# Turning a reversed block instead of copying mirrored filter rows: one change to a spectral filter that runs beside a gated MLP

## The chip, the cores and the metric

One NeuronCore of a Trainium2 chip runs the whole program. The metric is the device time of one execution in microseconds (us). Five engines work side by side, each on its own list of instructions in order: PE (TensorE, matrix products), DVE (VectorE), ACT (ScalarE), POOL (GpSimd) and SP (SyncE, which here only issues transfers). A lower time is better.

## The reference, cut to what matters

The output is the sum of the input, of a filter in the frequency domain and of a gated MLP, both on the layer-normed input. S is 2048 rows, D 512 columns, Df 1792; all arrays are bf16.

```python
def _A_ref(x, w_r, w_i):
    B, S, D = x.shape
    X = rfft2(x.astype(float32), axes=(-2, -1))
    W = w_r + 1j * w_i                       # (S, D // 2 + 1)
    X = X * W
    return irfft2(X, s=(S, D), axes=(-2, -1)).astype(bfloat16)

def _B_ref(x, w_gate, w_up, w_down):
    g = einsum("bsd,df->bsf", x, w_gate)
    u = einsum("bsd,df->bsf", x, w_up)
    h = gelu(g) * u
    return einsum("bsf,fd->bsd", h, w_down)

xn = layernorm(A_x, axis=-1)
return A_x + _A_ref(xn, A_w_r, A_w_i) + _B_ref(xn, B_w_gate, B_w_up, B_w_down)
```

## The kernel before

**A planner writes the order.** The program first records operations (`op`), each with an engine, a cost, a key and what it reads and writes. `_Sched.run` then walks through them with these costs, picks at each step the operation that can start first (the key decides between close ones, a `due` time overrides it), and adds `MARGIN`, 1 us, to the time at which a matmul counts as ready. What comes out is one fixed list for each engine. On the chip each engine follows its list; an instruction that finds its input missing holds everything behind it. So a changed cost or a new operation can move instructions that have nothing to do with it.

**The rows.** The 2048 rows are 16 tiles of 128, and four tiles make a block (blocks 0 to 3). For each tile `stats` (L524, L525) takes mean and variance, POOL or ACT makes the reciprocal root (L537, L531), and `norm` (L541) writes the normed rows to specB, in eight slots of 512 elements. A normed tile is transposed into xnT: tiles 0 to 3 on PE (`turn`, L554, copied out of PSUM in L559), tiles 4 to 15 by a transfer on SP's queue (`turn_dma`, L563).

**The MLP.** `gated` multiplies 128 rows of wg and of wu by xnT (L686, PE), ACT applies gelu (L691) and copies the other product (L692), and DVE multiplies both into hT (L693). gg and uu have four buffers each and ps_gu has three PSUM banks. Block 0 has 128-wide (`first`, L705) and 256-wide pieces first; all else is 512 wide. `down` (L731) multiplies by wd.

**The filter.** `fold` (L571) takes a block of xnT and makes the sums and differences of its four groups of 128 columns in f: two groups for the even channels, two for the odd ones; then it folds rows against their mirror rows into z (L584, L586). `f_c` (L597) multiplies z by cosines and sines (Tf): for each pair of tiles, two matmuls of 128 columns for the even channels and two of 256 for the odd ones, twice. ACT copies the result to specA (L602). When all 16 tiles are there, DVE does a 16-point transform across tiles (from L780 on), and PE the rest over 128 rows (`f_t`, L820 and L823). The spectrum X stands in eight classes of rows. For the product, DVE folds X to real and mirrored parts, multiplies by the filter W (`filt`, real and imaginary parts, near rows and mirrored "far" rows) in two halves of four classes each (L849 to L884), and PE and DVE go back the same way (`f_i` L900, L901; `f_b` L960), until the result is added to x and stored (L748). The last rows of the MLP (L731 into ps_sp) end the program.

**Transfers.** SP's queue carries, in this order: the x tiles and weights, the rest of `small` (288 KB of constants), x of blocks 2 and 3, four transposes, wd, six transposes, tokf, two transposes, then the filter. Its near rows are loaded straight (strided rows of 514 bytes). Its far rows are needed in reversed order: three transfers for each of w_r and w_i copy them reversed into a scratch tensor w_mirror in DRAM (L655 to L659), and six loads each bring them in from there. `toki`, constants for L900, stands between. The two small sums `edge` (L833, POOL) wait for the whole filter, and DVE uses them and W near the product.

```python
load("sp", small[:, 2:11].rs([9 * P]), c_small.ap()[:, 2 * P:], 294912, key=next(k))
...
for s in (2, 3):
    norm(s, -50.0)
    turn(s, 1, -50.0)
fold(0)
...
    turn_dma(s)
    if s % 4 == 3:
        fold(s // 4)
```

Of the kernel before, what the change touches and what calls it, by code (L numbers as in the profile page):

```python
# [9 lines left out]
BF16 = mybir.dt.bfloat16  # L10
# [3 lines left out]
D = 512  # L14
FF = 1792
P = 128
# [19 lines left out]

def _constants():
    npbf = mybir.dt.np(BF16)
    th = 2.0 * np.pi / S
    m = np.arange(P)  # L40
    K = np.zeros((8, P))
    K[0] = 8 * (2 * (m % 64) + m // 64)
    for v, c in enumerate((4, 1, 9, 2, 10, 3, 11)):
        K[v + 1] = c + 16 * m
    q = np.arange(P) + 0.5
    ph = th * q[:, None, None] * K[None]
    co, si = np.cos(ph), np.sin(ph)
    si2 = si.copy()
    si2[:, 0, 0] = np.sin(th * q * 1024)
    cof = co.copy()  # L50
    cof[:, 0, 0] *= 0.5
    low = (m < 64)[None]
    tf = []
    for a in (cof, si2):
        for part in (low, ~low):
            e = a[:64, 0] * part
            tf.append(np.concatenate([e, 0 * e] if a is cof else [0 * e, e]))
    for v, c in enumerate((4, 1, 9, 2, 10, 3, 11)):
        g = -1.0 if c > 8 else 1.0
        c = min(c, 16 - c)  # L60
        if c % 2:
            r = np.sin(np.pi * c / 2)
            f = r * g, r
        else:
            f = (-1.0, 1.0) if c == 4 else (g, -1.0)
        tf.append(np.concatenate([co[:64, v + 1], f[0] * si[:64, v + 1]]))
        tf.append(np.concatenate([g * co[:64, v + 1], f[1] * si[:64, v + 1]]))
    tf = np.stack(tf, 1)
    ci, sv = co[:64].transpose(2, 1, 0), si2[:64].transpose(2, 1, 0)
    sg = np.array([0, 1, 1, 1, 1, -1, -1, -1])[:, None]  # L70
    pr = np.concatenate([ci, -sg * sv], 2)
    pi = np.concatenate([sv, sg * ci], 2)
    lo = (m < 64)[:, None]
    for a in (pr, pi):
        half = a[:, 0, 0:64].copy()
        a[:, 0] = np.concatenate([half * lo, half * ~lo], 1)
    ti = np.stack([pr, pi, -pi], 2)
    a = 2.0 * np.pi / D * (np.arange(P) + 0.5)[:, None]
    ke = 2 * np.arange(P)[None]
    kse = ke.copy()  # L80
    kse[0, 0] = 256
    T = np.stack([np.cos(a * ke), np.cos(a * (ke + 1)), np.sin(a * kse), np.sin(a * (ke + 1))], 1)
    al = np.full((P, 4), 2.0)
    al[0, 0] = al[0, 2] = 1.0
    Ti = T.transpose(2, 1, 0) * al[:, :, None] / (S * D)
    fwd = []
    for d0, r in ((0, (0,)), (0, (2,)), (0, (1, 3)), (P, (1, 3))):
        kk = np.concatenate([np.arange(i, 256, 4) for i in r])[None]
        ks = np.where(kk == 0, 256, kk)
        a = 2.0 * np.pi / D * (d0 + np.arange(P) + 0.5)[:, None]  # L90
        fwd += [np.cos(a * kk), np.sin(a * ks)]
    small = np.concatenate([np.eye(P)] + fwd + [Ti.reshape(P, 512)], 1)

    def cvt(z):
        return np.ascontiguousarray(z.reshape(P, -1).astype(np.float32).astype(npbf))

    return cvt(small), cvt(tf), cvt(ti)
# [253 lines left out]
def bass_parallel_sum__spectral_gfnet__glu_gated_geglu__prompt_kernel(  # L351
# [26 lines left out]
    op = sch.op  # L378

    with ExitStack() as es:  # L380
# [22 lines left out]
        small = sb("smallc", [11, P])  # L403
        tf = sb("tokf", [18, P])
# [22 lines left out]
        Tf = small[:, 1:7]  # L427
        Ti = small[:, 7:11]
# [71 lines left out]
        load("sp", small[:, 2:11].rs([9 * P]), c_small.ap()[:, 2 * P:], 294912, key=next(k))  # L500
# [69 lines left out]

        def fold(b):  # L571
# [8 lines left out]
            tt(f[:, :, 2:4], xt[:, :, 0:2], xt[:, :, 2:4], SUB, 1024, kk)  # L580
# [6 lines left out]
            for p in {0: (), 1: (4, 6), 2: (8, 10), 3: (12, 14, 0, 2)}[b]:  # L587
                t = _T("sp")

                def f_c(e, p=p, t=t):  # L590
                    ins = None
                    for o in range(2):
                        bank = spb(t, o).rearrange("p (s r i) -> p s r i", s=2, r=4)
                        for cc in range(4):
                            to = bank[:, :, 2 * cc] if cc < 2 else bank[:, :, 1::2]
                            mat = Tf.ap[:, cc] if cc < 2 else Tf.ap[:, 2 * cc - 2:2 * cc]
                            ins = e.matmul(to, z.ap[:, p + o, cc, :], mat, start=(cc == 0), stop=(cc == 3))  # L597
                    return ins

                op("pe", 4 * 0.057 + 4 * 0.11, f_c, reads=(z[:, p:p + 2], Tf), tiles=(t,), key=kk, lag=0.1)  # L600
# [17 lines left out]
        for s in (2, 3):  # L618
            norm(s, -50.0)
            turn(s, 1, -50.0)  # L620
        fold(0)
# [5 lines left out]
        for s in range(4, 16):  # L627
            norm(s, 0.0, NORM[0] + NORM[1] * (s - 4))
            hold[s] = sch.ops[-1]
            turn_dma(s)  # L630
            if s % 4 == 3:
                fold(s // 4)
# [4 lines left out]
        load("sp", tf, c_tf.ap().rearrange("p (t m) -> p t m", t=18), 589824, key=next(k))  # L637
        for ri, src in ((0, A_w_r), (1, A_w_i)):
            r16 = src.rearrange("(m c) k -> m c k", c=16)
            load("sp", W[0:64, ri, 0, 0], r16[0:64, 0], 32896, key=next(k))  # L640
            load("sp", W[64:P, ri, 0, 0], r16[0:64, 8], 32896, key=next(k))
            load("sp", W[:, ri, 0, 1], r16[:, 4], 65792, key=next(k))
            for c in (1, 2, 3):
                load("sp", W[:, ri, 0, 2 * c:2 * c + 2], r16[:, c:c + 9:8], 131584, key=next(k))
            load("sp", W[0:1, ri, 1, 0], r16[0:1, 0], 514, key=next(k))
        op("pool", 0.1, lambda e: e.memset(w1[0:1].ap, 0.0), writes=(w1,))
        for dst, src, lo, hi in ((w1[0:1, 0, 0:256], A_w_r, 0, 256), (w1[0:1, 0, 257:512], A_w_i, 1, 256),
                                 (w1[0:1, 1, 1:256], A_w_i, 1, 256), (w1[0:1, 1, 257:512], A_w_r, 1, 256),
                                 (w1[0:1, 1, 256:257], A_w_r, 256, 257)):
            load("sp", dst, src[1024:1025, lo:hi], 512, key=next(k))  # L650
        gate.append(hold[15])
        scr, far, near = {}, {}, {}
        for ri, src in ((0, A_w_r), (1, A_w_i)):
            c16 = src.rearrange("(m c) k -> c m k", c=16)
            scr[ri] = nc.dram_tensor("w_mirror%d" % ri, (9, P, 257), BF16, kind="Internal").ap()  # L655
            far[ri] = [
                dma("sp", lambda ri=ri: scr[ri][0:4], lambda c16=c16: c16[12:16, ::-1, :], 526336, key=next(k), cost=3.5, lag=6.0),
                dma("sp", lambda ri=ri: scr[ri][5:8], lambda c16=c16: c16[5:8, ::-1, :], 394752, key=next(k), cost=2.5, lag=6.0)]
            near[ri] = dma("sp", lambda ri=ri: scr[ri][4:9:4, 0:64], lambda c16=c16: c16[0:9:8, 127:63:-1, :], 131584, key=next(k), cost=2.0, lag=5.0)  # L659
        load("sp", ti, c_ti.ap().rearrange("p (v t q) -> p v t q", v=8, t=3), 786432, key=next(k))  # L660
        for ri in (1, 0):
            load("sp", W[1:64, ri, 1, 0], scr[ri][4, 0:63], 32382, after=(near[ri],), key=1.0 + next(k))
            load("sp", W[64:P, ri, 1, 0], scr[ri][8, 0:64], 32896, after=(near[ri],), key=1.0 + next(k))
            load("sp", W[:, ri, 1, 1], scr[ri][0], 65792, after=(far[ri][0],), key=1.0 + next(k))
            for c in (1, 2, 3):
                load("sp", W[:, ri, 1, 2 * c:2 * c + 2], scr[ri][4 - c::4][0:2].rearrange("c m k -> m c k"), 131584, after=tuple(far[ri]), key=1.0 + next(k))
# [122 lines left out]
        u = Fb[:, 2:4]  # L789
        tt(u, s2[:, 0:2], s2[:, 2:4], ADD, 1024)  # L790
        tt(H[:, 14], u[:, 0], u[:, 1], ADD, 512)
        tt(H[:, 15], u[:, 0], u[:, 1], SUB, 512)
# [20 lines left out]
        for v, hh in enumerate(((14, 15), (12, 13), (0, 1), (4, 6), (8, 9), (10, 11), (2, 7), (5, 3))):  # L813
# [23 lines left out]
        for B in range(2):  # L837
            vs = slice(4 * B, 4 * B + 4)
# [5 lines left out]
            xh = R1(4096 * B, [4, 2, 2, 256])  # L844
# [27 lines left out]
            if B == 0:  # L872
                row = X[0:1, 0, 1]
                u1, u2 = M[0:1, 1].rs([2048])[:, 0:512], M[0:1, 1].rs([2048])[:, 512:1024]
                tt(u1, row, w1[0:1, 0], MUL, 512)
                tt(u2, row, w1[0:1, 1], MUL, 512)
# [11 lines left out]
        for v in range(8):  # L888
# [16 lines left out]
            gv = G[:, v].tr((1, 0, 2))  # L905
# [106 lines left out]
```

## Time and profile before

| | |
|---|---|
| median of three runs | 174.48 us (174.15 to 174.85) |
| the profiled execution | 173.99 us |
| its span, from the first to the last instruction | 172.2 us |
| granted TensorE clock | 1.00 |
| PE busy 8 to 22 us; 22 to 158 us | 13.71 of 14.00; all of it |
| DVE busy 22 to 52; 52 to 90; 90 to 130 us | 24.40 of 30; 35.24 of 38; 38.52 of 40 |
| DVE's wait for x of rows 8 to 11 | 0.44 us, until 20.87 |
| POOL's wait for the filter (L833) | 42.1 us, until 74.7 |
| landing of a transpose after issue | 3.2 to 7.1 us, median 4.2 |

How to read it: the span is what the profile covers; the time of the execution has some 1.8 us around it. The profile gives for each engine the time in which instructions ran, and for an idle stretch what released the next instruction. Matmuls overlap: one 512-wide matmul lasts 379 ns, yet the next one starts 216 ns after it. The list of the engine that is never idle sets the time. An instruction that follows others with no gap tells nothing of its own deadline.

### The profile page before, as it was taken

What the parts mean: (1) busy time and instruction counts of PE and PEld (TensorE: products, weight loads), DVE (VectorE), ACT (ScalarE), POOL (GpSimd) and SP (SyncE); (2) the same over time, 40 slices, a digit from 0 to 9 for tenths busy, and PEclk for the clock granted to TensorE, in tenths of its full rate; (3) what the DMA queues carried; (4) which work ended last, traced back from release to release, by engine and by line L of the source; (5) the groups of instructions that cost most, each with busy time, mean ns of one, the idle gap of its engine ahead of it and who ended that gap; (6) DMA issues with size and microseconds to landing.
All of it is one profiled execution on the core that took longest, in us unless ns stands there. A gap on an engine that the chain in (4) does not pass through costs nothing.

```text
span 172.2 us, 2683 instructions
## 1 busy us (share of the span) xinstructions
PE 167.9 (98%) x994; PEld 87.1 (51%) x994; DVE 143.3 (83%) x283; ACT 106.2 (62%) x172; POOL 11.8 (7%) x25
## 2 busy tenths in 40 slices
PE   7899999999999999999999999999999999999994
PEld 2588544455574444444444464554445664444443
DVE  2779899998539999967999999979999949972931
ACT  3378666675894647969645495794636996562000
POOL 2222234300000000030000000000000000000000
PEclk9999999999999999999999999999999999999999
DMA  5999999967532224920000000000000002410311
GB/s 150 299 356 354 298 145 300 231 151 144 122 81 63 61 52 97 308 71 4 0 2 0 0 4 0 0 0 0 4 0 2 0 4 81 129 36 0 122 64 61
DMA packets 24333, 16.35 MB, mean 95 GB/s; under 512 B 7679, under 2 KB 23936, under 8 KB 24320
## 3 DMA queue, kind: packets, MB, share of 16 engines
q1 hardware_dynamic: 23120, 15.32, 35.3%
q10 hardware_dynamic: 1200, 0.85, 1.6%
q8 instruction: 8, 0.13, 0.3%
q14 instruction: 5, 0.04, 0.1%
HBM read 12.50 MB, written 3.15 MB: 91 GB/s over the span
## 4 chain that ended last, share of the span: by engine, by line
PE 93%; DMA 4%; ACT 1%; DVE 1%; issue 0%; DVEq 0%
PE ps_gu L686 55%; PE ps_dn L731 21%; PE ps_sp L731 7%; DMA x_sb<-in_A_x_dram 4%; PE ps_sp L597 3%; PE ps_sp L960 2%; PE ps_sp L820 2%; PE ps_sp L900 1%; PE ps_sp L901 1%; ACT gg L716 1%; PE ps_sp L823 1%; DVE bst L524 0%; PE ps_gu L705 0%; PE ps_sp L554 0%; ACT uu L717 0%
## 5 line engine op out<-in xcount | busy, mean ns | idle before, releaser
L686 PE MATMUL ps_gu<-xnT,wu 128*128 128x512 bf16 (+1 forms) x236 | 56.7, 363 | 0.2 <-ACT gg L716 0.2
L686 PE MATMUL ps_gu<-xnT,wg 128*128 128x512 bf16 (+1 forms) x236 | 56.7, 363 | 0.0
L691 ACT ACTIVATE gg<-ps_gu 128x512 bf16<-128x512 f32 (+1 forms) x59 | 33.6, 570 | 13.1 <-PE ps_gu L686 10.4
L692 ACT ACTIVATE uu<-ps_gu 128x512 bf16<-128x512 f32 (+1 forms) x59 | 33.7, 572 | 10.8 <-PE ps_gu L686 10.5
L731 PE MATMUL ps_dn<-wd,hT 128*128 128x512 bf16 x168 | 38.9, 379 | 0.0
L686 PEld LDWEIGHTS ps_gu<-xnT,wg 128*128 128x128 bf16 x236 | 22.8, 98 | 22.9 <-DVE xnT L559 0.3
L686 PEld LDWEIGHTS ps_gu<-xnT,wu 128*128 128x128 bf16 x236 | 22.7, 98 | 22.9 <-ACT gg L716 0.4
L472 DVE TENSOR_TENSOR specB<-specB 128x1024 bf16<-128x1024 bf16 (+2 forms) x47 | 29.3, 662 | 1.5 <-ACT specB L965 1.4
L731 PEld LDWEIGHTS ps_dn<-wd,hT 128*128 128x128 bf16 x168 | 16.4, 98 | 19.1
L693 DVE TENSOR_TENSOR hT<-gg,uu 128x512 bf16<-128x512 bf16 (+1 forms) x59 | 22.5, 396 | 3.1 <-ACT uu L692 3.1
L739 ACT ACTIVATE db<-ps_dn 128x512 bf16<-128x512 f32 x12 | 7.2, 597 | 18.6 <-PE ps_dn L731 18.5
L524 DVE BATCH_NORM_STATS2 bst<-x_sb 128x6 f32<-128x512 bf16 x16 | 10.9, 685 | 3.6 <-DMA x_sb<-in_A_x_dram 3.6
L472 DVE TENSOR_TENSOR specC<-specB 128x1024 bf16<-128x1024 bf16 (+5 forms) x21 | 12.8, 634 | 0.2
L731 PE MATMUL ps_sp<-wd,hT 128*128 128x512 bf16 (+2 forms) x70 | 12.3, 336 | 0.0
L472 DVE TENSOR_TENSOR specB<-specA 128x2048 bf16<-128x2048 bf16 x8 | 9.4, 1220 | 2.9 <-ACT specA L602 2.4
L740 DVE TENSOR_TENSOR x_sb<-db,x_sb 128x512 bf16<-128x512 bf16 x12 | 5.0, 417 | 6.7 <-ACT db L739 6.7
L731 PEld LDWEIGHTS ps_sp<-wd,hT 128*128 128x128 bf16 x70 | 6.3, 97 | 6.1 <-DVE x_sb L742 0.2
L472 DVE TENSOR_TENSOR specB<-specB,filt 128x2048 bf16<-128x2048 bf16 x8 | 9.4, 1216 | 0.0
L828 ACT ACTIVATE specA<-ps_sp 128x1024 bf16<-128x1024 f32 x8 | 8.0, 1024 | 1.6 <-PE ps_sp L820 1.3
L602 ACT ACTIVATE specA<-ps_sp 128x1024 bf16<-128x1024 f32 x8 | 7.8, 1028 | 1.7 <-PE ps_sp L597 1.6
L965 ACT ACTIVATE specB<-ps_sp 128x1024 bf16<-128x1024 f32 x8 | 7.8, 1031 | 0.4 <-PE ps_sp L960 0.4
L906 ACT ACTIVATE specC<-ps_sp 128x1024 bf16<-128x1024 f32 x8 | 7.8, 1039 | 0.0
(64 smaller groups left out, 131.2 us busy)
## 6 DMA issues: line engine op xcount, KB each, us to landing
wd<-in_B_w_down_dram SPq DMA_DIRECT2D x1, 1792.0 KB, 8.8
out_dram<-x_sb SPq DMA_DIRECT2D x14, 128.0 KB, 1.8
x_sb<-in_A_x_dram SPq DMA_DIRECT2D x3, 512.0 KB, 8.8
wg<-in_B_w_gate_dram SPq DMA_DIRECT2D x2, 512.0 KB, 7.5
wu<-in_B_w_up_dram SPq DMA_DIRECT2D x2, 512.0 KB, 8.2
filt<-w_mirror SPq DMA_DIRECT2D x6, 128.5 KB, 5.2
toki<-c_ti SPq DMA_DIRECT2D x1, 768.0 KB, 7.9
tokf<-c_tf SPq DMA_DIRECT2D x1, 576.0 KB, 4.3
```

The source lines that it names most:

```text
L472: return op("dve", c_tt(n), lambda e: e.tensor_tensor(o.ap, a.ap, b.ap, f), reads=(a, b), writes=(o,), key=key, **kw)
L524: op("dve", 0.61, lambda e: e.bn_stats(bst[:, s].ap, xs(s).ap), reads=(xs(s),), writes=(bst[:, s],), key=key, due=due, after=after)
L602: op("act", c_act(1024), lambda e, yv=yv, t=t: e.activation(yv.ap, spair(t).rearrange("p (s r i) -> p s i r", s=4, r=4), ACT.Copy), writes ...
L686: ins = e.matmul(gub(t, n), w.ap[:, dc, fc * P:(fc + 1) * P], xnT.ap[:, b, sl, dc, :], start=(dc == 0), stop=(dc == 3))
L691: op("act", c_act(n), lambda e: e.activation(gg.ap[:, gs.slot, 0:n], gub(g, n), ACT.Gelu_apprx_tanh), tiles=(g, gs), key=0.0)
L692: op("act", c_act(n), lambda e: e.activation(uu.ap[:, us.slot, 0:n], gub(u, n), ACT.Copy), tiles=(u, us), key=0.0)
L693: op("dve", c_tt(n), lambda e: e.tensor_tensor(hT.ap[:, h.slot, lo:lo + n], gg.ap[:, gs.slot, 0:n], uu.ap[:, us.slot, 0:n], MUL), tiles=(g ...
L731: ins = e.matmul(bank(), hT.ap[:, hs[(b, fc)].slot, sl * P:(sl + 1) * P], wd.ap[:, fc, lo:lo + n], start=(fc == 0), stop=(fc == NFC - 1))
L739: op("act", c_act(n), lambda e: e.activation(db.ap[:, d.slot, 0:n], bank(), ACT.Copy), tiles=(t, d), key=0.0)
L828: op("act", c_act(1024), lambda e, xv=xv, t=t: e.activation(xv.ap, spair(t), ACT.Copy), writes=(xv,), tiles=(t,), key=-0.5)
L906: op("act", c_act(1024), lambda e, gv=gv, t=t: e.activation(gv.ap, spair(t).rearrange("p (k x i) -> p k x i", k=4, x=4), ACT.Copy), writes ...
L965: op("act", c_act(1024), lambda e, rv=rv, t=t: e.activation(rv.ap, spair(t), ACT.Copy), writes=(rv,), tiles=(t,), key=-0.5)
```

## The change

The frequencies of odd channels have a second symmetry: the columns 128 to 255 and 384 to 511, taken backwards, can be folded onto the first 128. Columns are partitions once a tile is transposed. The change takes the difference of these columns before the transpose, where they lie along the row and can be read backwards, and transposes this difference, 128 rows x 512 elements for a block, of its own (`mirror`): block 0 on PE with a copy out of PSUM, blocks 1 to 3 by a transfer on SP's queue. `fold` then makes the odd channels from the difference of columns 0 to 127 and 256 to 383 minus and plus this turned block. The matmuls of odd channels are then 128 wide instead of 256, and two constant matrices go.

For the filter, the lanes (partitions) of X run backwards: the row classes are numbered differently (`K`, and the constants made from it), so that the mirrored rows of the filter can be loaded straight from w_r and w_i. The scratch tensor and its loads go. For each of w_r and w_i there is one load of near rows (128 partitions, 7 channels together, 3,598 bytes a row), two of far rows (64 partitions, 7 rows of 514 bytes each), one of class 0's near rows and two of its far rows, and afterwards two single rows. w1, one partition before, now lies in partition 64 of a full tile, which is cleared whole. The classes change their order: the product takes the even ones (0, 2, 4, 6) first and then the odd ones, f_t makes them in the order 4, 0, 2, 6, 1, 7, 3, 5, and f_i runs over 0, 4, 1, 7, 2, 6, 3, 5.

In the lists that the planner writes for the changed kernel, mirror's transposes stand on SP's queue behind the transposes of tiles 9 and 13 and, for block 3, behind the first two filter loads (near rows of w_r, and a half of its far rows).

```diff
-        small = sb("smallc", [11, P])
+        small = sb("smallc", [9, P])
...
-        Tf = small[:, 1:7]
-        Ti = small[:, 7:11]
+        Tf = small[:, 1:5]
+        Ti = small[:, 5:9]
...
-        load("sp", small[:, 2:11].rs([9 * P]), c_small.ap()[:, 2 * P:], 294912, key=next(k))
+        load("sp", small[:, 2:9].rs([7 * P]), c_small.ap()[:, 2 * P:], 229376, key=next(k))
...
+        odd = {}
+
+        def mirror(b):
+            rows = RB(8192 + 2048 * (b % 2), [4, 4, P])
+            g = RB(2048 * (b % 2) + 1024, [4, P])
+            odd[b] = RB(2048 * (b % 2) + 1536, [4, P])
+            tt(g, rows[:, :, 1, ::-1], rows[:, :, 3, ::-1], SUB, 512, 0.5)
+            if b:
+                op("sp", 1.25, lambda e: e.dma_start_transpose(odd[b].ap, g.rs([512]).ap), reads=(g,), writes=(odd[b],), dma=425000, key=-5.0)
+                return
+            t = _T("sp")
+
+            def bank():
+                return ps_sp_bf[:, t.slot * 2048:t.slot * 2048 + 512]
+
+            def f(e):
+                for i in range(4):
+                    ins = e.transpose(bank()[:, i * P:(i + 1) * P], g.ap[:, i], ident.ap)
+                return ins
+
+            op("pe", 4 * 0.056, f, reads=(g, ident), tiles=(t,), key=2.0, lag=0.1)
+            op("dve", 0.34, lambda e: e.tensor_copy(odd[b].rs([512]).ap, bank()), writes=(odd[b],), tiles=(t,), key=1.0)
...
-            tt(f[:, :, 2:4], xt[:, :, 0:2], xt[:, :, 2:4], SUB, 1024, kk)
+            tt(f[:, :, 3], xt[:, :, 0], xt[:, :, 2], SUB, 512, kk)
+            tt(f[:, :, 2], f[:, :, 3], odd[b], SUB, 512, kk)
+            tt(f[:, :, 3], f[:, :, 3], odd[b], ADD, 512, kk)
...
                         for cc in range(4):
-                            to = bank[:, :, 2 * cc] if cc < 2 else bank[:, :, 1::2]
-                            mat = Tf.ap[:, cc] if cc < 2 else Tf.ap[:, 2 * cc - 2:2 * cc]
-                            ins = e.matmul(to, z.ap[:, p + o, cc, :], mat, start=(cc == 0), stop=(cc == 3))
+                            to = bank[:, :, 2 * cc] if cc < 2 else bank[:, cc - 2, 1::2]
+                            ins = e.matmul(to, z.ap[:, p + o, cc, :], Tf.ap[:, cc], start=(cc == 0), stop=(cc == 3))
...
+        mirror(0)
         fold(0)
...
             if s % 4 == 3:
+                mirror(s // 4)
                 fold(s // 4)
...
+        gate.append(hold[15])
         for ri, src in ((0, A_w_r), (1, A_w_i)):
-            r16 = src.rearrange("(m c) k -> m c k", c=16)
-            load("sp", W[0:64, ri, 0, 0], r16[0:64, 0], 32896, key=next(k))
-            load("sp", W[64:P, ri, 0, 0], r16[0:64, 8], 32896, key=next(k))
-            load("sp", W[:, ri, 0, 1], r16[:, 4], 65792, key=next(k))
-            for c in (1, 2, 3):
-                load("sp", W[:, ri, 0, 2 * c:2 * c + 2], r16[:, c:c + 9:8], 131584, key=next(k))
-            load("sp", W[0:1, ri, 1, 0], r16[0:1, 0], 514, key=next(k))
-        op("pool", 0.1, lambda e: e.memset(w1[0:1].ap, 0.0), writes=(w1,))
...
+            near = src.rearrange("(a b c) k -> a b (c k)", a=2, b=64)[:, ::-1, 257:8 * 257]
+            far = src.rearrange("(a b c) k -> a b c k", a=2, b=64)
+            load("sp", W[:, ri, 0, 1:8], near, 460544, key=next(k))
+            for h in range(2):
+                load("sp", W[64 * h:64 * h + 64, ri, 1, 1:8], far[1 - h, :, 15:8:-1], 230272, key=next(k))
+            load("sp", W[:, ri, 0, 0], src[8:1032].rearrange("(b a c) k -> a b c k", a=2, c=8)[:, ::-1, 0], 65792, key=next(k))
+            for h in range(2):
+                load("sp", W[64 * h:64 * h + 64, ri, 1, 0], far[1, :, 8 - 8 * h], 32896, key=next(k))
+        for ri, src in ((0, A_w_r), (1, A_w_i)):
+            for i in range(2):
+                load("sp", W[64:65, ri, i, 0], src[0:1], 514, key=next(k))
+        op("pool", 0.6, lambda e: e.memset(w1.ap, 0.0), writes=(w1,))
...
-        gate.append(hold[15])
-        scr, far, near = {}, {}, {}
-        for ri, src in ((0, A_w_r), (1, A_w_i)):
-            c16 = src.rearrange("(m c) k -> c m k", c=16)
-            scr[ri] = nc.dram_tensor("w_mirror%d" % ri, (9, P, 257), BF16, kind="Internal").ap()
-            far[ri] = [
-                dma("sp", lambda ri=ri: scr[ri][0:4], lambda c16=c16: c16[12:16, ::-1, :], 526336, key=next(k), cost=3.5, lag=6.0),
-                dma("sp", lambda ri=ri: scr[ri][5:8], lambda c16=c16: c16[5:8, ::-1, :], 394752, key=next(k), cost=2.5, lag=6.0)]
-            near[ri] = dma("sp", lambda ri=ri: scr[ri][4:9:4, 0:64], lambda c16=c16: c16[0:9:8, 127:63:-1, :], 131584, key=next(k), cost=2.0, lag=5.0)
...
-        for ri in (1, 0):
-            load("sp", W[1:64, ri, 1, 0], scr[ri][4, 0:63], 32382, after=(near[ri],), key=1.0 + next(k))
...
-        u = Fb[:, 2:4]
-        tt(u, s2[:, 0:2], s2[:, 2:4], ADD, 1024)
-        tt(H[:, 14], u[:, 0], u[:, 1], ADD, 512)
-        tt(H[:, 15], u[:, 0], u[:, 1], SUB, 512)
+        tt(H[:, 14:16], s2[:, 0:2], s2[:, 2:4], ADD, 1024)
...
-        for v, hh in enumerate(((14, 15), (12, 13), (0, 1), (4, 6), (8, 9), (10, 11), (2, 7), (5, 3))):
+        for v, hh in ((4, (12, 13)), (0, (14, 15)), (2, (8, 9)), (6, (10, 11)), (1, (0, 1)), (7, (4, 6)), (3, (2, 7)), (5, (5, 3))):
...
-            vs = slice(4 * B, 4 * B + 4)
+            vs = slice(B, 8, 2)
...
-        for v in range(8):
+        for i, v in enumerate((0, 4, 1, 7, 2, 6, 3, 5)):
```

More of the change, by code (lines that the diff above doesn't have):

```diff
@@ L41, in _constants @@
     K = np.zeros((8, P))
-    K[0] = 8 * (2 * (m % 64) + m // 64)
-    for v, c in enumerate((4, 1, 9, 2, 10, 3, 11)):
-        K[v + 1] = c + 16 * m
+    mm = 63 - m + 128 * (m // 64)
+    K[0] = np.where(m < 64, 8 + 16 * mm, 16 * (128 - m) * (m != 64))
+    for c in range(1, 8):
+        K[c] = c + 16 * mm
     q = np.arange(P) + 0.5
@@ L48, in _constants @@
     si2 = si.copy()
-    si2[:, 0, 0] = np.sin(th * q * 1024)
+    si2[:, 0, 64] = np.sin(th * q * 1024)
     cof = co.copy()
-    cof[:, 0, 0] *= 0.5
+    cof[:, 0, 64] *= 0.5
     low = (m < 64)[None]
@@ L54, in _constants @@
     for a in (cof, si2):
-        for part in (low, ~low):
+        for part in (1, np.where(low, -1, 1)):
             e = a[:64, 0] * part
             tf.append(np.concatenate([e, 0 * e] if a is cof else [0 * e, e]))
[L58 to L67, printed above, removed]
+    for c in range(1, 8):
+        r = np.sin(np.pi * c / 2)
+        f = (r, r) if c % 2 else (-1.0, 1.0) if c == 4 else (1.0, -1.0)
+        tf.append(np.concatenate([co[:64, c], f[0] * si[:64, c]]))
+        tf.append(np.concatenate([co[:64, c], f[1] * si[:64, c]]))
     tf = np.stack(tf, 1)
     ci, sv = co[:64].transpose(2, 1, 0), si2[:64].transpose(2, 1, 0)
-    sg = np.array([0, 1, 1, 1, 1, -1, -1, -1])[:, None]
+    sg = np.array([0, 1, 1, -1, 1, 1, 1, -1])[:, None]
     pr = np.concatenate([ci, -sg * sv], 2)
@@ L75, in _constants @@
         half = a[:, 0, 0:64].copy()
-        a[:, 0] = np.concatenate([half * lo, half * ~lo], 1)
+        a[:, 0] = np.concatenate([half * ~lo, half * lo], 1)
     ti = np.stack([pr, pi, -pi], 2)
@@ L86, in _constants @@
     fwd = []
[L87 to L91, printed above, removed]
+    a = 2.0 * np.pi / D * (np.arange(P) + 0.5)[:, None]
+    for r in (0, 2):
+        kk = np.arange(r, 256, 4)[None]
+        fwd += [np.cos(a * kk), np.sin(a * np.where(kk == 0, 256, kk))]
+    odd = np.concatenate([np.arange(1, 256, 4), np.arange(3, 256, 4)])[None]
+    fwd += [np.cos(a * odd), np.sin(a * odd)]
     small = np.concatenate([np.eye(P)] + fwd + [Ti.reshape(P, 512)], 1)
@@ L594, in f_c @@
                         for cc in range(4):
-                            to = bank[:, :, 2 * cc] if cc < 2 else bank[:, :, 1::2]
-                            mat = Tf.ap[:, cc] if cc < 2 else Tf.ap[:, 2 * cc - 2:2 * cc]
-                            ins = e.matmul(to, z.ap[:, p + o, cc, :], mat, start=(cc == 0), stop=(cc == 3))
+                            to = bank[:, :, 2 * cc] if cc < 2 else bank[:, cc - 2, 1::2]
+                            ins = e.matmul(to, z.ap[:, p + o, cc, :], Tf.ap[:, cc], start=(cc == 0), stop=(cc == 3))
                     return ins
-                op("pe", 4 * 0.057 + 4 * 0.11, f_c, reads=(z[:, p:p + 2], Tf), tiles=(t,), key=kk, lag=0.1)
+                op("pe", 8 * 0.057, f_c, reads=(z[:, p:p + 2], Tf), tiles=(t,), key=kk, lag=0.1)
                 yv = Y[:, p:p + 2].rs([4, 64, 4])
@@ L645, in bass_parallel_sum__spectral_gfnet__glu_gated_geglu__prompt_kernel @@
-            load("sp", W[0:1, ri, 1, 0], r16[0:1, 0], 514, key=next(k))
-        op("pool", 0.1, lambda e: e.memset(w1[0:1].ap, 0.0), writes=(w1,))
-        for dst, src, lo, hi in ((w1[0:1, 0, 0:256], A_w_r, 0, 256), (w1[0:1, 0, 257:512], A_w_i, 1, 256),
-                                 (w1[0:1, 1, 1:256], A_w_i, 1, 256), (w1[0:1, 1, 257:512], A_w_r, 1, 256),
-                                 (w1[0:1, 1, 256:257], A_w_r, 256, 257)):
-            load("sp", dst, src[1024:1025, lo:hi], 512, key=next(k))
@@ L660, in bass_parallel_sum__spectral_gfnet__glu_gated_geglu__prompt_kernel @@
-        load("sp", ti, c_ti.ap().rearrange("p (v t q) -> p v t q", v=8, t=3), 786432, key=next(k))
-        for ri in (1, 0):
-            load("sp", W[1:64, ri, 1, 0], scr[ri][4, 0:63], 32382, after=(near[ri],), key=1.0 + next(k))
[L663 to L666, printed above, removed]
+            near = src.rearrange("(a b c) k -> a b (c k)", a=2, b=64)[:, ::-1, 257:8 * 257]
@@ new lines, in bass_parallel_sum__spectral_gfnet__glu_gated_geglu__prompt_kernel @@
+        for ri, src in ((0, A_w_r), (1, A_w_i)):
+            for i in range(2):
+                load("sp", W[64:65, ri, i, 0], src[0:1], 514, key=next(k))
+        op("pool", 0.6, lambda e: e.memset(w1.ap, 0.0), writes=(w1,))
+        for dst, src, lo, hi in ((w1[64:65, 0, 0:256], A_w_r, 0, 256), (w1[64:65, 0, 257:512], A_w_i, 1, 256),
+                                 (w1[64:65, 1, 1:256], A_w_i, 1, 256), (w1[64:65, 1, 257:512], A_w_r, 1, 256),
+                                 (w1[64:65, 1, 256:257], A_w_r, 256, 257)):
+            load("sp", dst, src[1024:1025, lo:hi], 512, key=next(k))
@@ L842, in perm @@
                 return v.tr((1, 0, 2))
-            xh = R1(4096 * B, [4, 2, 2, 256])
+            xh = R1(0, [8, 2, 2, 256])[:, vs]
             f0 = perm(xb_[:, :, :, 0:256])
@@ L872, in bass_parallel_sum__spectral_gfnet__glu_gated_geglu__prompt_kernel @@
             if B == 0:
[L873 to L876, printed above, removed]
+                row = X[64:65, 0, 1]
+                u1, u2 = M[64:65, 1].rs([2048])[:, 0:512], M[64:65, 1].rs([2048])[:, 512:1024]
+                tt(u1, row, w1[64:65, 0], MUL, 512)
+                tt(u2, row, w1[64:65, 1], MUL, 512)
             tt(g0, M[:, 0::2, 0], M[:, 0::2, 1], ADD, 2048)
@@ L904, in bass_parallel_sum__spectral_gfnet__glu_gated_geglu__prompt_kernel @@
             op("pe", 8 * 0.057, f_i, reads=(X[:, v], ti[:, v]), tiles=(t,), lag=0.1)
-            gv = G[:, v].tr((1, 0, 2))
+            gv = G[:, i].tr((1, 0, 2))
             op("act", c_act(1024), lambda e, gv=gv, t=t: e.activation(gv.ap, spair(t).rearrange("p (k x i) -> p k x i", k=4, x=4), ACT.Copy),
```

## The prediction

> **What bounds the kernel now.** I read the chain of waits first, then the groups by form, then a stretch of the timelines near 20 us and the transfer queue near 40 to 60 us.
>
> ```profile
> PE 167.9 (98%) x994; PEld 87.1 (51%) x994; DVE 143.3 (83%) x283; ACT 106.2 (62%) x172; POOL 11.8 (7%) x25
> PE 93%; DMA 4%; ACT 1%; DVE 1%; issue 0%; DVEq 0%
> ```
>
> The chain is PE almost from 8 us on. So PE's own work sets the end, and DVE's 83% costs nothing until an instruction on PE's list finds its input missing. Whatever PE saves is gained, and whatever PE is made to wait is lost. The saving is in these groups (line, shape, count, total, mean):
>
> ```profile
> L597 PE MATMUL ps_sp<-smallc,specC 128*128 128x256 bf16 x32 | 5.5, 273 | 0.0
> L597 PE MATMUL ps_sp<-smallc,specC 128*128 128x128 bf16 x32 | 4.4, 219 | 0.0
> L472 DVE TENSOR_TENSOR specB<-specB 128x512 bf16<-128x512 bf16 x16 | 6.1, 416 | 0.0
> ```
>
> Matmuls overlap, so I price them from start to start: the chain has sixteen of L597, half of each width, in 1.32 us and twelve 512-wide L686 in 2.59 us, which makes 0.056, 0.109 and 0.216 us for 128, 256 and 512 columns. DVE the same way: 0.335 us for 512 elements, 0.605 for 1024, 0.61 for BATCH_NORM_STATS2, 0.31 for the norm of L541, 0.21 for a 256-wide product.
>
> **The change, part by part.**
>
> *PE.* The 32 wide matmuls of L597 become 128 wide: 32 x (0.109 - 0.056) = 1.70 us less. Four transposes of block 0's reversed rows are added: 4 x 0.056 = 0.22. PE's short waits on copies and products before 20 us (0.22) go, since the new order does the two copies of L559 before the statistics of row 4. Alone: -1.70 + 0.22 - 0.22 = -1.7 us (-1.65 when I add up PE's list from 18.6 us on).
>
> *DVE.* Each block gets a 512 difference of reversed rows, and one 1024 difference becomes three of 512: 4 x (4 x 0.335 - 0.605) = +2.9, one copy +0.33, and L790 to L792 lose two 512 operations and keep one 1024: -0.67. Reversed reading costs nothing in the trace: the sums of L584 and L586, one input reversed, take 687 ns for 1024, plain ones 680. Both reversed is not shown; bounds 0 and another 0.27 us each (the 1024 price for 512); I take 0. All this lies under PE, except where it moves a product.
>
> *Where it moves a product, at 20 us.*
>
> ```profile
> 18.75 0.89 DVE L693 TENSOR_TENSOR hT<-gg,uu 128x256 bf16<-128x256 bf16 x4
> 20.87 0.69 DVE L524 BATCH_NORM_STATS2 bst<-x_sb 128x6 f32<-128x512 bf16 x1 [0.44 <-DMA x_sb<-in_A_x_dram]
> ...
> 19.64 0.60 ACT L691 ACTIVATE gg<-ps_gu 128x512 bf16<-128x512 f32 x1
> ...
> 21.24 1.03 PE L686 MATMUL ps_gu<-xnT,wu 128*128 128x512 bf16 x4
> ```
>
> DVE waited here for x of rows 8 to 11, after four products (L693) that free gg buffers. In the changed order only one of those four stands ahead of that statistic; the next is behind it. DVE reaches the statistic near 19.6. The load queued ahead is 64 KB shorter; at the 358 GB/s of 16 to 20 us this is 0.18, so x lands near 20.7. Then 0.61 (statistic) + 0.31 (norm) + 0.09 + 0.29 (product) gives 22.0; the gelu that needs this buffer runs to 22.6, and PE's u product of the second 512-wide unit, which needs that PSUM bank, starts at 22.65 instead of 21.21. Price 1.44 us. It falls to 0 if x landed at 19.2.
>
> *SP's queue and the filter.* The reversed blocks 1 to 3 go through three more transposes on SP, and the filter is loaded by other descriptors: the mirror copies in DRAM (L655 to L659) and their twelve loads go. The third new transpose stands behind two of the new loads.
>
> ```profile
> 36.15 2.54 SPq L563 DMA_TRANSPOSE xnT<-specB  x2
> 38.73 4.36 SPq L468 DMA_DIRECT2D filt<-in_A_w_r_dram  x7
> 48.55 6.20 SPq L468 DMA_DIRECT2D w_mirror<-in_A_w_r_dram  x3
> ```
>
> SP issues one transpose per 1.28 us here. Two stand ahead of the first filter load, 38.73 + 2.6 = 41.3; the down weights go out up to 1 us later too (behind norms 6 and 7). I take 41.5.
>
> ```profile
> 16.00:20.00 4.00, 4.00 (x33) 2.86 (x31) 3.90 (x14) 2.94 (x9) 1.57 (x3) 1.00 1.09 358
> 32.00:36.00 4.00, 4.00 (x20) 1.83 (x19) 4.00 (x11) 2.79 (x5) 0.55 (x1) 1.00 1.01 147
> 52.00:60.00 8.00, 8.00 (x39) 3.60 (x38) 7.94 (x11) 4.56 (x8) 0.00 (x0) 1.00 0.25 59
> ```
>
> The last two numbers are the busy share of 16 transfer engines and GB/s. In 52 to 60 only the mirror copies run. Their sources are patterns of 4 x 128, 3 x 128 and 2 x 64 rows, and 0.25 of 16 is four engines: the outer count seems to be the number of engines used. The new near load (channels 1 to 7 of w_r, 128 rows of 3,598 bytes) has a source of 2 x 64 rows. So two engines carry it, 230 KB each. One engine makes 358/16 = 22.4 GB/s on long rows, hence 10.3 us; the bounds are 386/16 (29 to 30 us) with 9.5 us and the mirror copies' 59/4 = 14.8 with 15.6 us. I take 22.4, as its rows are long and end in SBUF.
>
> [...]
>
> Transposes fill all engines (1.01 at only 147 GB/s, 32 to 36 us), and they queue behind what is ahead: the first one landed 6.7 us after issue behind the x loads, the fourth after 3.2. So the third new transpose ends when two engines have finished near: 41.5 + 1.6 (a 64 KB filter load lands 2.1 after issue, less its bytes and receipt) + 10.3 + 0.8 (28 short rows of the load between, at 29 ns: the first engine took 640 such rows of the mirror copies from 48.6 to 67 us) + 1.3 (itself) + 0.3 = 55.8 us. DVE reaches its reader, the third difference of block 3, near 48.9 by the prices above and holds there; behind it stand a product, another difference and the 1024 fold: 55.8 + 3 x 0.335 + 0.605 + 0.1 = 57.5. PE's first L597 pair of block 3 needs that fold; PE would come to it at 52.4 without stalls, at 53.8 after the stall at 20 us. So the second wait takes the first one in: 57.5 - 52.4 = 5.1.
>
> *The rest.* The filter itself: two near loads in a row on the same engines, with the shorter loads between them, end near 75 (43.1 + 2 x 10.3 + some 11 for what else these engines carry); the edge product that needs it on DVE comes after 80, so 5 us cover it. A 128-wide memset of w1 replaces a 1-wide one on POOL (942 ns now) long before use: 0. The order of product and inverse classes moves ACT and PE work by up to 2 us, with readers planned 1 us (MARGIN) behind their inputs: 0, bounds -0.3 and +1.
>
> **Sum.** PE's list from that pair on is 115.7 us by the prices: 57.5 + 115.7 = 173.2, where before's list ends at 169.8 in the same way. That is -1.65 + 5.1 = +3.4 us on the profiled span of 172.2 and its time of 173.99: 177.4. The median of the three runs is 0.49 above the profiled one, so I forecast 177.9.
>
> **Rivals.**
> (1) *Near is spread over all engines* (its 128 rows in SBUF count, not the source's 2). Then the transpose lands near 48, nobody waits, and only the stall at 20 us stays: -1.65 + 1.44 = -0.2, 174.3. For it: the earlier loads of filt into 128 rows land in 2.8 us. Against: the first mirror copy has 512 rows on its written side and still shows four engines.
> (2) *Faster: the late product finds cover.* With near spread as in (1), the product behind the statistic is all that is left; if x of rows 8 to 11 lands before 19.2, gelu has its buffer in time and the -1.65 stays whole: 172.8. For it: PE is never short of a buffer after 20 us now, and the queue ahead of x shrinks. Against: x landed at 20.87, and 64 KB are 0.18 us, not 1.6.
> (3) *Two engines at the mirror copies' rate.* Near takes 15.6 us: 5.3 more, 183.2; the edge product then stalls DVE too, up to 3 us, partly covered. For it: that is the only rate seen on so few engines. Against: there both ends were DRAM and the rows 514 bytes.
> (4) *PE comes back slow.* The ten 512-wide warm-up matmuls (L511) take 4.45 us, 0.43 each against 0.216 later, though the granted clock reads 1.00 throughout. If 3.7 us of idle put PE back there for ten matmuls, +2.1: 180.0. No idle over 1.2 us is in the trace to tell. [...]
>
> **How the numbers follow.** Forecast 0.48; (4) 0.14; (3) 0.15; (1) 0.12; (2) 0.11. The likeliest alone spans 176.9 (9.5 us for near, SP as early as 41.3) to 180.0 (18.6 GB/s, the middle of the two rates, 12.4 us). The range 174.0 to 183.0 leaves out (2) and half of (3), 0.19. Under 0.5% (0.87 us) this kernel's runs, 0.7 us apart, can't be told from no change. Slower: 0.48 + 0.14 + 0.15 = 0.77; same 0.12; faster 0.11.
>
> **What would show it.** Right: L597's successor with 64 matmuls near 219 ns and none at 273; DVE idle about 1 us before the statistic near 20.7 and PE idle over 1 us near 21 to 22.7; transfer share near 0.13 from about 44 to 53; DVE idle some 6 us, released by a transfer into specB, and PE idle some 4 us near 54 to 57.5. Wrong: a high transfer share at 42 to 45 (rival 1); no PE idle at 54; the long idle elsewhere, above all at the edge product near 80, which would mean that the filter and not the transpose is late.

## The result, and the profile after

The changed kernel takes 180.5 us (median of four runs, 179.79 to 181.38) against 174.31: a ratio of 1.0354, 95% interval 1.0315 to 1.0393. The forecast was 177.9, in a range of 174.0 to 183.0. The profiled execution took 181.13 us, its span is 179.3. The four executions fall into two pairs: 181.13 and 181.38 us with a mean granted clock of 0.981, and 179.79 and 179.86 with 0.99.

From the page of the changed kernel: the busy line, the granted clock in 40 slices of 4.5 us, the chain by engine, and the group that took the place of L597.

```profile
PE 168.8 (94%) x998; PEld 87.4 (49%) x998; DVE 146.0 (81%) x294; ACT 106.0 (59%) x172; POOL 12.2 (7%) x25
...
PEclk9999999999998589999999999999999999999999
...
PE 76%; DMA 13%; SPq 5%; ACT 2%; DVE 2%; issue 0%
...
L619 PE MATMUL ps_sp<-smallc,specC 128*128 128x128 bf16 x64 | 5.7, 253 | 4.5 <-DVE specC L470 4.5
```

PE's share of the chain fell from 93% to 76%, and transfers have 13%. All 64 forward matmuls are 128 wide now, as the change says, but their mean is 253 ns and not 219, and 4.5 us of idle time stand before them. The clock has a hole a third of the way through, which the rows further down place at 57 to 64 us.

The chain of waits has two places where it leaves PE (start, duration, what):

```profile
12.55 8.49 DMA x_sb<-in_A_x_dram
21.06 0.69 DVE bst L522
21.75 0.31 DVE specB L539
...
22.16 0.19 DVE hT L707
22.36 0.61 ACT gg L705
23.02 12.26 PE ps_gu L700 x56
...
43.93 12.96 DMA specB<-specB
56.92 0.43 DVE specB L470
57.34 0.34 DVE hT L707
57.68 0.35 DVE specB L470
58.05 0.70 DVE specC L470
58.80 1.89 PE ps_sp L619 x16
```

The first is the product near 20 us. It goes from x of rows 8 to 11 over the statistic, the norm and the product to gelu and PE, step by step as in the prediction. The second is the third transpose of the reversed rows. It was issued at 43.93 and landed at 56.92, and the difference, the product, the second difference and the fold of 1024 follow.

Three instructions from the timelines of SP, DVE and PE (start, duration, engine, what; in brackets the idle time before and what ended it), and then PE's clock around them (each row: stretch; its length and busy time of PE, PEld, DVE, ACT, POOL; clock; share of 16 transfer engines; GB/s):

```profile
43.93 6.91 SPq L577 DMA_TRANSPOSE specB<-specB  x1
...
56.92 0.43 DVE L470 TENSOR_TENSOR specB<-specB 128x512 bf16<-128x512 bf16 x1 [7.51 <-DMA specB<-specB]
...
58.80 1.89 PE L619 MATMUL ps_sp<-smallc,specC 128*128 128x128 bf16 x16 [4.47 <-DVE specC L470]
```

```profile
48.00:50.00 2.00, 2.00 (x20) 1.24 (x18) 1.41 (x5) 2.00 (x3) 0.00 (x0) 1.00 0.12 50
50.00:52.00 2.00, 2.00 (x11) 0.87 (x9) 0.00 (x0) 1.87 (x4) 0.00 (x0) 1.00 1.26 52
...
54.00:56.00 2.00, 0.33 (x2) 0.00 (x0) 0.00 (x0) 0.60 (x1) 0.00 (x0) 1.00 0.15 29
56.00:58.00 2.00, 0.00 (x0) 0.00 (x0) 1.08 (x3) 0.00 (x0) 0.00 (x0) 0.71 0.97 143
58.00:60.00 2.00, 1.20 (x12) 1.21 (x13) 1.97 (x5) 0.13 (x1) 0.00 (x0) 0.50 0.46 115
...
62.00:64.00 2.00, 2.00 (x12) 1.25 (x11) 2.00 (x2) 0.72 (x1) 0.00 (x0) 0.58 0.56 131
```

From 48 to 52 us only 50 to 52 GB/s move. In the clean row, 48 to 50, the share of 0.12 is two of 16 engines, 25 GB/s each. (The share of 1.26 beside 52 GB/s counts packets of other transfers that were begun and then stood: in the trace some of 256 bytes begin at 47.1 us and end at 56.1. Where bytes and share disagree, the bytes tell what went on.) PE stops at 54.3. Some 2.5 us later, in the row from 56 to 58, the clock begins to drop to 0.50, and it stays there until about 63.7, so that PE comes back to its work at half speed: the four 512-wide matmuls that start at 60.68 take 1.71 us, 0.43 each instead of 0.216.

### The profile page after: what moved, and what is told of

It is laid out like the page before. It is cut to its first block, busy times and chain, and to the rows that moved or that the text cites. A ratio compares the mean times of both kernels' runs of the same rounds, so it can differ in the third digit from the quotient of the medians.

```text
span 179.3 us, 2682 instructions
## 1 busy us (share of the span) xinstructions
PE 168.8 (94%) x998; PEld 87.4 (49%) x998; DVE 146.0 (81%) x294; ACT 106.0 (59%) x172; POOL 12.2 (7%) x25
## 4 chain that ended last, share of the span: by engine, by line
PE 76%; DMA 13%; SPq 5%; ACT 2%; DVE 2%; issue 0%
PE ps_gu L700 44%; PE ps_dn L745 18%; DMA specB<-specB 7%; PE ps_sp L745 7%; DMA x_sb<-in_A_x_dram 6%; SPq L466 5%; PE ps_sp L971 2%; PE ps_sp L619 2%; PE ps_sp L831 2%; PE ps_sp L911 1%; ACT specA L624 1%; PE ps_sp L912 1%; ACT gg L705 1%; PE ps_sp L834 0%; DVE specB L470 0%
## 5 line engine op out<-in xcount | busy, mean ns | idle before, releaser
L700 PE MATMUL ps_gu<-xnT,wg 128*128 128x512 bf16 (+1 forms) x236 | 57.6, 367 | 0.0
L470 DVE TENSOR_TENSOR specB<-specB 128x512 bf16<-128x512 bf16 (+2 forms) x58 | 33.3, 610 | 9.0 <-DMA specB<-specB 7.5
L470 DVE TENSOR_TENSOR specC<-specB 128x1024 bf16<-128x1024 bf16 (+4 forms) x20 | 12.7, 659 | 0.3
L619 PE MATMUL ps_sp<-smallc,specC 128*128 128x128 bf16 x64 | 5.7, 253 | 4.5 <-DVE specC L470 4.5
L619 PEld LDWEIGHTS ps_sp<-smallc,specC 128*128 128x128 bf16 x64 | 5.0, 115 | 6.2 <-DVE specC L470 5.0
```

Source lines behind the costliest of these rows:

```text
L470: return op("dve", c_tt(n), lambda e: e.tensor_tensor(o.ap, a.ap, b.ap, f), reads=(a, b), writes=(o,), key=key, **kw)
L619: ins = e.matmul(to, z.ap[:, p + o, cc, :], Tf.ap[:, cc], start=(cc == 0), stop=(cc == 3))
L700: ins = e.matmul(gub(t, n), w.ap[:, dc, fc * P:(fc + 1) * P], xnT.ap[:, b, sl, dc, :], start=(dc == 0), stop=(dc == 3))
```

## Experiments

In all of them the engines' lists are those of the changed kernel but for the entries named, so that nothing else is planned anew. The baseline measured beside them was 174.25 us for the first four and 174.32 for the last three.

### The third transpose ahead of the near load

```
         sch.run()
+        sp = sch.order["sp"]
+        sp.insert(31, sp.pop(33))       # transpose of block 3's reversed rows, ahead of filt's first two loads
```

> The changed kernel with one entry of SP's list moved: the third reversed block's transpose is issued ahead of the first near load of w_r instead of two loads behind it; every other engine keeps its list. My theory (the transpose is late because it queues behind 461 KB that only two transfer engines carry): it lands near 47 instead of 56.9, the third difference of block 3 on DVE doesn't wait, PE has no idle time at 54 to 59 and the clock stays at 1.00. That takes away 4.5 us of idle and the 2.5 us after it: 180.5 - 6.5 = 174.0 (173.6 to 175.2, the upper end if the filter, now one transpose later, holds the edge product on DVE near 79). Rival, the filter's near loads are late for their own readers: the wait only moves to the edge product, 176 to 178. Rival, transposes are slow whatever stands ahead: landing stays over 52, time above 177.

174.41 us (10 runs, 173.75 to 176.06); ratio to before 1.001 (0.9984 to 1.0036). SP's queue in the timeline of this kernel, and the stretch in which PE stood still before (columns as above):

```profile
42.58 1.26 SPq L577 DMA_TRANSPOSE specB<-specB  x1
43.89 13.46 SPq L466 DMA_DIRECT2D filt<-in_A_w_r_dram  x6
```

```profile
54.00:56.00 2.00, 2.00 (x22) 1.28 (x20) 0.43 (x1) 1.53 (x3) 0.00 (x0) 1.00 0.12 50
56.00:58.00 2.00, 2.00 (x22) 1.40 (x22) 1.07 (x1) 2.00 (x3) 0.00 (x0) 1.00 0.22 50
```

The transpose is issued in 1.26 us instead of 6.91. Nothing on DVE waits for it, PE is busy all through, the clock stays at 1.00, and two engines still move the near load at 50 GB/s, now in nobody's way. One move in one queue is worth 6.1 us. DVE waits 0.19 us for the edge sums at 78.8, so the filter has not become the bound.

### PE kept busy in the wait

```
         sch.run()
+        pair = min((pairs[p] for p in (12, 14, 0, 2)), key=pe.index)
...
+        for _ in range(16):
+            f = sch.op("pe", 0.0, lambda e: e.matmul(spb(t, 0), zero.ap[:, 0:P], zero.ap, start=True, stop=True))
+            f.preds, f.end = early, pair.end
+            pe.insert(i, f)
```

> The changed kernel with 16 matmuls of zeros, 512 wide (16 x 0.216 = 3.5 us), put on PE ahead of the first forward pair of block 3, into the PSUM bank that this pair overwrites; they don't wait for DVE, so PE works through most of the 4.5 us in which it was idle. All else keeps its place. Theory: the transpose still lands near 57 and the pair still starts near 58.8, but the granted clock stays at 1.00, and the 2.5 us by which PE's list behind the pair ran longer than before go: 180.5 - 2.0 (mean clock of the four runs: half with 0.981, half with 0.99) = 178.5 (178.0 to 179.0). Rival, that lateness is DVE's and ACT's backlog after the wait and not the clock: no change, 180.5.

178.2 us (177.97 to 178.42); ratio 1.0224 (1.0201 to 1.0247). PE's timeline:

```profile
53.85 3.62 PE L999 MATMUL ps_sp<-zero 128*128 128x512 bf16 x16
58.36 1.07 PE L619 MATMUL ps_sp<-smallc,specC 128*128 128x128 bf16 x16 [0.89 <-DVE specC L470]
```

The pair starts at 58.36 (58.80 without the zeros; the transpose landed at 56.48 here), and its sixteen matmuls take 1.07 us instead of 1.89. The clock is 1.00 throughout. Behind the start of the pair PE's list takes 115.9 us, where the changed kernel took 118.2. Useless work on PE made the kernel 2.3 us faster by the medians; between the two profiled executions it is 2.8, of which 0.4 is the earlier start of the pair. That is what the clock costs, and the wait alone leaves it at 178.2.

### The products near 20 us ahead of the statistic

```
+        d = sch.order["dve"]
+        for a, b in ((46, 43), (48, 44)):     # two products, ahead of the statistic of row tile 8
+            d.insert(b, d.pop(a))
```

> The changed kernel with two entries of DVE's list moved: the two 256-wide products that free gelu buffers near 20 us stand ahead of the statistic that waits for x of rows 8 to 11, as four of them did before. Theory: PE's 1.2 to 1.3 us of idle before 23.0 goes, but PE then only comes earlier to the forward pair of block 3, whose input is set by the transpose at 56.9: idle there grows from 4.5 to about 5.8, and the time stays within 0.5 us of the changed kernel's 180.5. Rival, the two waits add up: 179.2.

180.53 us (179.71 to 181.11), the changed kernel's time. PE's first wait is gone (4.00 of 4.00 us busy from 20 to 24, 2.83 in the changed kernel). The second one grew, as PE's line in the waits shows (what was waited for, us in total, times, longest):

```profile
PE ps_sp L619 <- DVE specC L470: 5.9, 1, 5.9
```

The pair starts at 58.60. The clock was at 0.50 here from 54.86 to 61.69, again for 6.8 us, but more of it fell into the wait: behind the start of the pair PE's list took 117.3 us and not 118.2. Ahead of the longer wait this one cost nothing: taking it away alone brought nothing, 180.53 against 180.5.

### Both moves

> Both moves at once: the third transpose ahead of the near load, and the two products ahead of the waiting statistic. Theory: with the second wait gone the first one counts, so this move is now worth its 1.3 us: what is left is the 1.65 us of matmul work saved, 174.3 - 1.65 = 172.7 (172.2 to 173.4). Rival, the filter becomes the bound: the edge sums on POOL end at 79.5 and DVE would reach their reader near 77, 2.5 us of wait on DVE, of which PE feels up to 2: 174.7.

173.05 us (6 runs, 172.59 to 173.8); ratio 0.9933 (0.991 to 0.9956). It is the first version that is faster than the kernel before, by 1.2 us, and the products' move that was worth nothing above is worth 1.36 here (174.41 to 173.05). The edge sums are ready just in time (DVE's timeline):

```profile
77.41 0.29 DVE L878 TENSOR_TENSOR edge<-specA,edge 128x16 bf16<-128x16 bf16 x2 [0.19 <-POOL edge L844]
```

So the 2.5 us of the rival did not come. The sums were there at 77.4 and not at 79.5; the two POOL instructions took 0.73 us in all, where the changed kernel's profile showed 2.7. Why they were shorter isn't known.

### Fewer bytes ahead of the transpose

```
-            load("sp", W[:, ri, 0, 1:8], near, 460544, key=next(k))
+            parts = [load(... [:, ::-1, 257 * lo:257 * hi], 65792 * (hi - lo), ...) for lo, hi in ((1, 7), (7, 8))]
+            tail = tail if ri else parts[1]
...
+        sp.remove(tail)
+        sp.insert(sp.index(turned[3]) + 1, tail)
```

The second kernel has `((1, 5), (5, 8))` in that place.

> The changed kernel with the near loads cut by channel: six of the seven channels (395 KB, still 2 x 64 source rows) where the load stood, the seventh behind the third transpose. Same bytes, same order of all other work. Theory (two engines at 50 GB/s together stand ahead of the transpose): 66 KB less ahead are 1.3 us, so it lands near 55.6 and PE's idle time before block 3's first forward pair shrinks from 4.5 to about 3.2 us. The clock fell 2.5 us after PE went idle, so it should still fall: 180.5 - 1.3 = 179.2 (178.6 to 179.6); if 3.2 us are too short for it, 176.9. Rival, the transpose waits for a fixed time on SP's queue whatever the size ahead: 180.5.

> The same cut after four channels: 263 KB ahead of the third transpose, three channels (197 KB) behind it. Theory: 197 KB at 50 GB/s are 3.9 us, the transpose lands near 53.0, PE idles about 0.6 us there and the clock stays at 1.00: 174.4 (the version with the transpose wholly ahead) + 0.5 = 174.9 (174.2 to 175.5). Rival, a fixed time on the queue: 180.5.

With six channels ahead 177.8 us (four runs from 176.8 to 179.54; ratio 1.0205, 1.0131 to 1.028), with four 174.81 (ratio 1.0033, 1.0012 to 1.0055). Each kernel's SP and DVE timelines, six channels first:

```profile
43.87 5.97 SPq L577 DMA_TRANSPOSE specB<-specB  x1
...
55.03 0.43 DVE L470 TENSOR_TENSOR specB<-specB 128x512 bf16<-128x512 bf16 x1 [5.63 <-DMA specB<-specB]
...
56.91 1.07 PE L619 MATMUL ps_sp<-smallc,specC 128*128 128x128 bf16 x16 [2.59 <-DVE specC L470]
```

```profile
43.61 3.14 SPq L577 DMA_TRANSPOSE specB<-specB  x1
...
52.98 0.43 DVE L470 TENSOR_TENSOR specB<-specB 128x512 bf16<-128x512 bf16 x1 [3.75 <-DMA specB<-specB]
...
54.86 1.07 PE L619 MATMUL ps_sp<-smallc,specC 128*128 128x128 bf16 x16 [0.71 <-DVE specC L470]
```

461, 395 and 263 KB ahead give landings at 56.92, 55.03 and 52.98: 197 KB are 3.94 us, which is 50 GB/s, the rate of two engines at 25. (The steps are uneven: 1.9 us for the first 66 KB, where 1.3 were expected, and 2.05 for the next 132, where 2.6 were. In the traces the load itself ends at 54.36, 53.28 and 50.39, so part of the unevenness arose behind it, and the cause of that stays open.) A fixed time in the queue is refuted.

With six channels the time lies outside the expected range, between two outcomes. In the execution shown PE idled 2.59 us and the clock stayed at 1.00, at 176.9 us, and one more took 176.8. The other two read 0.99 on average and took 178.71 and 179.54; how long PE idled in them is not on record. The expectation that the clock would fall was right for some executions only.

The clock's times in the traces suggest why. It was at 0.50 for 6.83 us in the changed kernel (56.86 to 63.69) and with the products moved (54.86 to 61.69), which is twice 3.41 us, and the stretches at 1.00 before that, 51.2 and 47.8 us, are 15 and 14 times 3.41. So in these two traces the clock changed on a grid of 3.41 us. Here is the stretch of this grid in which PE stopped: in the changed kernel, with the products moved, and with six channels ahead (counted from the first record of its clock, at 4.31 us).

```profile
53.45:56.86 3.41, 0.88 (x5) 0.19 (x2) 0.00 (x0) 0.60 (x1) 0.00 (x0) 1.00 0.39 79
```

```profile
51.45:54.86 3.41, 1.27 (x6) 0.39 (x4) 0.00 (x0) 0.60 (x1) 0.00 (x0) 1.00 1.16 51
```

```profile
52.09:55.51 3.42, 2.23 (x10) 0.79 (x9) 0.48 (x2) 0.60 (x1) 0.00 (x0) 1.00 0.23 45
```

Behind the first two, in which PE worked 0.88 and 1.27 us, the clock fell. Behind the third, with 2.23, and the one after it, with 2.01, it did not. That the work in such a stretch decides is a reading of three traces and not a test. It would fit the rest: the same idle time can leave much or little work in a stretch, by where it falls. And a mean clock of 0.99 over some 178 us is about one such stretch at 0.50, and 0.981, the mean of the two traces with 6.83 us, is two.

### The near load with a plain outer dimension

```
-            near = src.rearrange("(a b c) k -> a b (c k)", a=2, b=64)[:, ::-1, 257:8 * 257]
+            near = src.rearrange("(m c) k -> m (c k)", c=16)[:, 257:8 * 257]
```

> The changed kernel with the two near loads reading their 128 rows in plain order, one outer dimension of 128 instead of 2 x 64 reversed; same rows, bytes and place in the queue. It leaves out the reversal of the filter's near rows, so these lanes are multiplied by other rows' filter values. Theory (the outer count of the source sets the number of engines): 16 engines carry it at a busy share near 1 and over 200 GB/s in some 2 us instead of 11, the transpose lands before 49, nobody waits, 174.4 (173.8 to 175.0). Rival, it is the long rows or the size of the load and not the outer count: no change, 180.5.

173.96 us (10 runs, 173.64 to 174.99); ratio 0.9989 (0.9967 to 1.001). SP's queue and the stretch of the load:

```profile
41.67 1.29 SPq L466 DMA_DIRECT2D filt<-in_A_w_r_dram  x2
43.01 1.30 SPq L577 DMA_TRANSPOSE specB<-specB  x1
```

```profile
44.00:46.00 2.00, 2.00 (x11) 0.91 (x10) 1.85 (x5) 1.01 (x3) 0.00 (x0) 1.00 1.16 268
```

Rows, bytes and place are the same. All transfers together move 268 GB/s from 44 to 46, 119 in the changed kernel; in the trace the load itself lasts 2.2 us instead of 10.4. DVE doesn't wait, and the filter is complete 15 us sooner (POOL's wait for it is 29.3 us instead of 44.5). So it was the form of the pattern and not the size, the rows or the place. The plain pattern differs in two ways, one dimension of 128 for 2 x 64 and rows in forward order, and no run parts them. The mirror copies of the kernel before speak for the count: they read reversed rows too, with outer counts of 4, 3 and 2, and ran at a share of 0.25, some four engines.

## Why the prediction was right, and where it was short

- **What bounds the kernel.** PE's list, and waits on it. Right: with both waits taken out and nothing else, 173.05.
- **The saving on PE, -1.65.** Seen as -1.2 with both waits out. In that profile PE waited 0.69 us at 11 us for ACT, where the kernel before waited 0.15; in two other executions of changed versions this wait was absent. It may be the rest; that wasn't tested. The prediction had wiped out 0.22 us of short waits there instead.
- **Reversed reading.** Both inputs reversed: 0.39 to 0.42 us for 512 elements, the plain price (0.416 on average in the kernel before). The value of 0 was right.
- **The wait at 20 us, 1.44 us.** The same chain. PE went on at 23.02, not 22.65, as x landed at 21.06 instead of 20.7. In the profiles with one or both moves it landed at 21.16, 20.92 and 20.68, so a gain of 0.18 from 64 KB less in front of it can't be made out. That it is swallowed by the second wait was right, and shown by moving the products alone.
- **Two engines for near.** Right in effect, and in cause as far as the runs show it. In the trace the load lasted 10.4 us (43.91 to 54.36), 10.3 predicted, but that fit is in part luck: an engine made 25.0 GB/s where the load ran alone, 22.4 assumed, and less before 48 us. That the outer count of the source sets the number of engines was the author's estimate from the mirror copies and their share of 0.25. The runs fit it and don't prove it: a share of 0.12 and 50 GB/s with 2 x 64 rows, and with 128 in plain order a load of 2.2 us instead of 10.4.
- **The landing at 55.8.** It was 56.92. SP reached near at 42.51 instead of 41.5, which is most of the 1.1 us. Near's faster rate was used up before 48 us: 37 of its 128 rows had come by then, in 4.1 us, and the other 91 took 6.4. From 44 to 48 all transfers together moved 106 to 119 GB/s, so others probably shared its engines. Two small terms of that sum, the receipt taken off the 2.1 us and the 0.3 at its end, are shown singly by no run. In their place the trace has 1.4 us from the issue to near's first packet, 1.6 assumed, and 2.56 from near's end to the landing, 2.4 assumed. From landing to pair 1.9 us, 1.7 predicted.
- **PE coming back at full speed.** Here the forecast failed. "-1.65 + 5.1" priced PE's list behind the pair at 115.7 us; in the profile it took 118.2 (58.80 to 177.0). With zeros in the wait and the clock at 1.00 it took 115.9, so the price was right but for the clock, which the idle time of 4.5 us, 3.7 predicted, had lowered. That was rival (4), 0.14, priced at +2.1; the zeros on PE measure 2.3. Its time, 180.0, is close to the one that came, and its reason was the right one: PE came back with 512-wide matmuls 0.43 us apart, as in the warm-up. The weight was wrong: by the forecast's own sum PE idled 3.7 us, and the rival was held down for want of any idle time over 1.2 us in the trace. So the range held the result with room for this rival in it, and not by the forecast's own path. PE wasn't idle all through the 3.41 us ahead of the two drops: it worked 0.88 and 1.27 us of them.
- **The sum.** In the profiled execution 181.13 - 177.4 = 3.7: landing 1.1, chain to the pair 0.2, clock 2.5, which add up but for 0.1. The median of the four executions is 2.6 above the forecast.
- **The filter.** Predicted near 75, it came at 76.8 and held nobody in the changed kernel. Right.
- **The other rivals.** Near spread wide (1) is what the plain pattern gives, 461 KB in 2.2 us, or 209 GB/s, and 173.96 against 174.3 worked out: the case was sized well, its condition didn't hold. The faster case (2) needs x before 19.2; x came at 21. The slow rate (3) is refuted by the 10.4 us of the load, against 15.6.

## What to carry to other kernels

Before a load is rewritten to larger rows, look at the outer dimension that the new pattern leaves: here 2 x 64 rows went over two engines at 50 GB/s, and the transpose queued behind them landed 13.0 us after its issue. A load that may come late belongs behind a transfer that something is about to need, a move worth 6.1 us here. And price a stall on the matmul engine with what follows it: stalls of 4.5 and 5.9 us brought a slow restart with them, and one of 2.6 us did not in the execution shown, so that cheap filler in the wait, or one move in a queue, can be worth more than the work that the change was made to save.

## What the runs showed of the hardware

- An idle PE of 4.5 us (5.9 in one run) lowered the clock to 0.50 from 2.5 us (2.1) after it stopped, for 6.83 us in both runs, until 4.9 us (3.1) after work had come back: 2.3 us in all by the medians. At idle times of 0.7 and 0.9 us the clock stayed at 1.00, and at 2.59 us too in the execution shown, while others of that kernel read 0.99.
- In both traces with a drop, the times at which the clock changed lie multiples of 3.41 us apart (51.2 and 6.83 us, 47.8 and 6.83), and it fell behind stretches in which PE had worked 0.88 and 1.27 us. Whether that work decides, and how little of it would do, was not tested.
- The issue itself was held up. The transpose behind the near load took SP 6.91, 5.97 and 3.14 us to issue with 461, 395 and 263 KB on two engines ahead of it, and 1.26 to 1.30 us with none ahead or with the load in plain order. SP passed on nothing else while it stood there (in the changed kernel the next load went out at 50.88, right behind it), so the slow load also delayed the issue of what followed in its queue.
